# Two early expert slots in place of one in a fused attention, mixture-of-experts and FFN kernel

## The chip, the cores and the metric

The kernel runs on one core of a Trainium2 chip. The metric is the device time of one execution in microseconds (us). Engines are named as in the profile: PE is TensorE (PEld its weight loads), DVE is VectorE, ACT is ScalarE, POOL is GpSimd, SP is SyncE, which issues most transfers.

## The reference

Three stages follow one another. All inputs are float32.

```
attention:  q, k, v [4, 8, 576, 64]; scores / 8, masked by blocks of 64, softmax, times v
            -> x [2304, 512]                      (4 batches of 576 tokens, 8 heads of 64)
experts:    logits = x @ w_gate                   (8 experts)
            e(n) = argmax logits[n];  g(n) = softmax(logits[n])[e(n)]
            y[n] = g(n) * (relu(x[n] @ w1[e(n)]) @ w2[e(n)])     w1 [8, 512, 1024], w2 [8, 1024, 512]
FFN:        h = y @ w_in;  out = (relu(h) + log1p(exp(-|h|))) @ w_out    w_in [512, 2048], w_out [2048, 512]
```

So each token goes to one expert only, and which one is known when the attention of its batch, and its logits, are done.

## The kernel before

**Order of the work.** One long text, `SCHEDULE` (L45), lists some 3700 short keys in the order in which their instructions are written out. Each engine runs its own instructions in that order and waits where an input isn't there. So a key's place in the text is its place in the queue of its engine, for SP's transfers and POOL's gathers too.

**Attention.** 16 pairs of heads (4 batches, 4 pairs each). A pair `p` has keys such as `Kta.p` (transposes), `S0.p` to `S2.p` (scores), `m..p` (row maxima on DVE), `e..p` (exponentials on ACT), `T`, `h` (transposes of the weights and their copies), `V.p` (product with v), `Xa.p`, `xa.p`, `xo.p` (tokens and logits out; `xs` is stored to `xd` in device memory, L444). The pairs overlap. PSUM tile `ps2` has one buffer, which scores, token output and routing share.

**Routing.** Tokens are put into slots of 256 (`SR`), each for one expert. The early routing (`early_routing`, L610, keys `er0` to `er51`) works on the first two batches, beside the attention of the last pairs: it picks the expert with the most tokens there (`est`, L653), ranks its tokens, and makes a table of the first 256 (`giE` which token, `siE` where it goes, `gaE` its gate). Three of its steps are matmuls (count L631, ranks L636, table L641), the others short DVE operations. The late routing (`late_routing`, L693, keys `lr0` to `lr50` and `lg0` to `lg21`) starts when the attention ends; it counts all tokens that are left by expert (`oh` has 9 groups, group 0 the left tokens of the early expert), makes tables for the late slots (L750 for the token numbers, L746 for position and gate, the latter from five POOL products at L738 into `r_X`), and writes the expert of each slot and whether it differs from that of the slot ahead into `fl`.

**Slots.** Slot 0 is the early one; slots 1 to 11 are late (`NSTAT` = 12 run always; `more_slots`, L1402, runs a further one only if the late tables need it, and reads their number on every engine, L1404 in the profile). A slot `s` has these keys: `d10+s` to `d23+s` load the expert's weights, 8 x 512 KB on SP into `R` (L875, L877; from slot 1 on a load is left out when `fl` says the expert is the same); `h1i+s`, `h2i+s` on ACT (L880) and `l1i+s`, `l2i+s` on DVE (L884) split them into a high and a low part; `g0+s`, `g1+s` gather 128 tokens each on POOL (L888); `X`, `xh`, `xl` transpose and split the tokens (L903, L907, L911); `A0+s` to `A3+s` are the first layer (three products, L921 to L923), `hh`, `hl` its relu split (L927, L931); `C0+s` to `C7+s` the second layer (L941 to L943); `yo`, `sc` scale the result (L947) and scatter it (a one-column copy L951, an indirect transfer L952). Each weight part has one buffer, so slot s+1's conversions follow slot s's last use of it. The pools of the first layer's parts open near the end of the attention (`mp`), those of the second layer after it (`lp`). Keys `v0+f` to `v5+f` convert blocks of `w_in` for the FFN beside slots 1 to 4 (L840 to L845), and `vd+f` loads them (L823).

**FFN.** It follows the slots and is not touched by the change.

Of the kernel before, what the change touches and what calls it, by code (L numbers as in the profile page):

```python
# [9 lines left out]
BF16 = mybir.dt.bfloat16  # L10
I32 = mybir.dt.int32
# [11 lines left out]
SR = 256  # L23
NE, NSTAT, NSLOT = 2, 12, 16
# [89 lines left out]
h27+1 hl0+1 A1+1 d22+2 lg19 lg20 l26+1 lg21 more v0+0 l27+1 h10+2 v1+0 d23+2 h12+2 l10+2 A2+1 h14+2 l12+2 hh1+1 v2+0
h16+2 hl1+1 v0+1 v3+0 vd+2 l14+2 A3+1 v4+0 l16+2 hh2+1 v5+0 hl2+1 h11+2 v1+1 h13+2 l11+2 X0+2 h15+2 C0+1 l13+2 hh3+1
d10+3 xh0+2 l15+2 d11+3 h17+2 hl3+1 C1+1 h20+2 xl0+2 d12+3 v0+2 l17+2 X1+2 h21+2 l20+2 d13+3 C2+1 g0+3 xh1+2 l21+2
xl1+2 d20+3 g1+3 h22+2 C3+1 v2+1 l22+2 h23+2 C4+1 v3+1 vd+3 l23+2 v4+1 v1+2 C5+1 h24+2 d21+3 v5+1 l24+2 h25+2 C6+1
v2+2 l25+2 v3+2 vd+4 h26+2 C7+1 d22+3 v0+3 l26+2 v1+3 A0+2 yo0+1 sc0+1 v2+3 yo1+1 v3+3 vd+5 h27+2 v4+2 l27+2 sc1+1
v4+3 v5+2 d23+3 A1+2 v0+4 v5+3 hh0+2 v1+4 hl0+2 h10+3 v2+4 h12+3 l10+3 A2+2 h14+3 l12+3 hh1+2 l14+3 h16+3 hl1+2 v0+5
l16+3 v3+4 vd+6 A3+2 hh2+2 v1+5 v4+4 hl2+2 v0+6 v5+4 v2+5 v1+6 X0+3 C0+2 v3+5 vd+7 hh3+2 C1+2 xh0+3 v2+6 h11+3 hl3+2  # L120
h13+3 X1+3 xl0+3 h15+3 C2+2 g0+4 l11+3 xh1+3 l13+3 h17+3 d10+4 g1+4 C3+2 xl1+3 h20+3 d11+4 h21+3 l15+3 h22+3 l17+3
d12+4 C4+2 h23+3 l20+3 v4+5 d13+4 l21+3 v0+7 C5+2 l22+3 d20+4 h24+3 l23+3 h25+3 C6+2 l24+3 d21+4 l25+3 v5+5 h26+3
d22+4 C7+2 v3+6 vd+8 yo0+2 sc0+2 l26+3 A0+3 h27+3 v1+7 yo1+2 l27+3 v4+6 sc1+2 v2+7 d23+4 v5+6 v3+7 c9.-1 A1+3 hh0+3
v4+7 hl0+3 v0+8 v5+7 v1+8 h10+4 v2+8 h12+4 A2+3 hh1+3 l10+4 h14+4 hl1+3 h16+4 l12+4 l14+4 l16+4 A3+3 hh2+3 v3+8 c10.-1
hl2+3 v4+8 h11+4 v5+8 h13+4 l11+4 X0+4 h15+4 l13+4 C0+3 d10+5 hh3+3 l15+4 xh0+4 d11+5 hl3+3 h17+4 C1+3 h20+4 xl0+4
d12+5 l17+4 h21+4 X1+4 l20+4 d13+5 C2+3 g0+5 xh1+4 l21+4 xl1+4 d20+5 g1+5 h22+4 C3+3 l22+4 h23+4 C4+3 l23+4 h24+4
d21+5 C5+3 l24+4 h25+4 C6+3 l25+4 h26+4 d22+5 C7+3 l26+4 yo0+3 sc0+3 A0+4 h27+4 yo1+3 l27+4 sc1+3 d23+5 A1+4 hh0+4
hl0+4 h10+5 h12+5 l10+5 A2+4 h14+5 l12+5 hh1+4 l14+5 h16+5 hl1+4 l16+5 A3+4 hh2+4 hl2+4 h11+5 h13+5 l11+5 X0+5 h15+5
l13+5 C0+4 d10+6 hh3+4 l15+5 xh0+5 d11+6 hl3+4 h17+5 C1+4 h20+5 xl0+5 d12+6 l17+5 h21+5 X1+5 l20+5 d13+6 C2+4 g0+6
xh1+5 l21+5 xl1+5 d20+6 g1+6 h22+5 C3+4 l22+5 h23+5 C4+4 l23+5 h24+5 d21+6 C5+4 l24+5 h25+5 C6+4 l25+5 h26+5 d22+6  # L130
# [363 lines left out]
def routing_consts(tc, const, B):  # L494
# [38 lines left out]
    for n in ("sel", "nsel"):  # L533
        t(n, [128, E])
# [314 lines left out]
def moe(tc, P, K, R1, R2, xd, yd, w1, w2, w_in, HB, ident):  # L849
# [612 lines left out]
```

## Time and profile before

| | |
|---|---|
| time, median of 3 runs | 965.75 us (965.72 to 967.75) |
| the profiled execution's own time | 966.58 us |
| its span, first to last instruction | 964.9 us |
| granted TensorE clock, mean | 0.980 |
| TensorE busy | 911.9 us (95%) |
| VectorE busy | 665.9 us (69%) |
| ScalarE busy | 567.1 us (59%) |
| GpSimd busy | 142.0 us (15%) |
| moved | 144.98 MB, mean 150 GB/s |

Matmuls overlap in the array, so a row's duration is longer than the distance to the next row; where a sum is made, the distance from start to start counts. In a row of the order of time, the bracket gives the idle time of the engine ahead of it and what ended it. Slot starts, by the first L921 row after a second layer: slot 0 at 237.46 us, slot 2 at 303.33 us, slot 4 at 361.39 us, slot 5 at 384.73 us.

### The profile page before, as it was taken

How to read it: one execution, taken by the hardware profiler on the slowest of the kernel's cores; microseconds unless marked ns; L12 is line 12 of the kernel's file. 1: busy time of each engine (PE TensorE's matmuls, PEld its weight loads, DVE VectorE, ACT ScalarE, POOL GpSimd, SP SyncE). 2: the span in 40 equal slices, each digit the busy share in tenths (PEclk: the TensorE clock that was granted, in tenths of full speed). 3: DMA queues.
4: the chain of work that ended last, by engine and by line, in shares of the span. 5: the costliest groups of instructions: out<-in, count | busy, mean ns of one | idle time of the engine just before them, and what ended most of it. 6: DMA issues, size and time to landing. Idle time of an engine off the chain costs nothing.

```text
span 964.9 us, 18308 instructions
## 1 busy us (share of the span) xinstructions
PE 911.9 (95%) x6331; PEld 804.0 (83%) x6331; DVE 665.9 (69%) x1454; ACT 567.1 (59%) x1256; POOL 142.0 (15%) x183
## 2 busy tenths in 40 slices
PE   6999999999868989999999999999999989999994
PEld 4888888767757979999999887888788989999994
DVE  3776677886877966655655277777666559897873
ACT  3766766765355755555555287888788733444331
POOL 2000000010244312222221100000000003130401
PEclk9999999999979989999999999999999999999997
DMA  5973630061117773466611167556664583433421
GB/s 128 200 148 76 127 81 26 25 210 47 51 54 248 235 250 132 155 239 231 209 52 62 44 202 217 187 184 229 231 251 185 186 339 105 149 129 121 130 70 64
DMA packets 132982, 144.98 MB, mean 150 GB/s; under 512 B 70415, under 2 KB 91919, under 8 KB 132880
## 3 DMA queue, kind: packets, MB, share of 16 engines
q1 hardware_dynamic: 127600, 127.98, 42.8%
q0 software_dynamic: 5280, 15.75, 4.8%
q8 instruction: 51, 0.84, 0.4%
q14 instruction: 51, 0.42, 0.1%
HBM read 120.09 MB, written 41.96 MB: 168 GB/s over the span
## 4 chain that ended last, share of the span: by engine, by line
PE 60%; DMA 4%; DVE 3%; ACT 1%; issue 1%; SPq 0%; POOLq 0%; ACTq 0%; DVEq 0%
PE yps L941 4%; PE yps L942 4%; PE yps L943 4%; PE hps L921 3%; PE hps L922 3%; PE hps L923 3%; PE fh L1085 3%; PE fh L1084 3%; PE fh L1086 3%; PE fz L1248 2%; PE fz L1247 2%; DMA gq<-gd 2%; PE fz L1246 2%; PE fX L1085 2%; PE fX L1086 2%; PE fX L1084 2%
## 5 line engine op out<-in xcount | busy, mean ns | idle before, releaser
L921 PE MATMUL hps<-xh,H1h 128*128 128x256 f32 x384 | 110.9, 289 | 6.5 <-ACT y L947 2.9
L922 PE MATMUL hps<-xl,H1h 128*128 128x256 f32 x384 | 110.4, 288 | 5.2 <-DVE xl L911 5.2
L1209 ACT CAST ah<-sum 128x1280 fp32r<-128x1280 f32 (+1 forms) x40 | 46.3, 1156 | 113.0 <-DVE sum L1202 55.4
L923 PE MATMUL hps<-xh,H1l 128*128 128x256 f32 x384 | 110.1, 287 | 0.0
L383 ACT ACTIVATE P<-s,negm 128x448 f32<-128x448 f32 (+4 forms) x160 | 82.8, 528 | 24.4 <-DVE negm L378 24.4
L884 DVE TENSOR_TENSOR H2l<-R,H2h 128x512 fp32r<-128x512 f32 x96 | 64.8, 694 | 34.2 <-ACT H2h L880 30.8
L378 DVE TENSOR_REDUCE negm<-s 128x1 f32<-128x576 f32 (+4 forms) x160 | 67.9, 478 | 22.3 <-PE s L372 21.0
L941 PE MATMUL yps<-H2h,hh 128*128 128x512 f32 x192 | 78.3, 408 | 3.8 <-DVE hl L931 3.8
L921 PEld LDWEIGHTS hps<-xh,H1h 128*128 128x128 f32 x384 | 75.2, 196 | 7.6 <-ACT y L947 3.1
L922 PEld LDWEIGHTS hps<-xl,H1h 128*128 128x128 f32 x384 | 75.2, 196 | 6.1 <-DVE xl L911 5.7
L884 DVE TENSOR_TENSOR H1l<-R,H1h 128x512 fp32r<-128x512 f32 x96 | 66.7, 738 | 17.7 <-ACT H1h L880 16.7
L942 PE MATMUL yps<-H2h,hl 128*128 128x512 f32 x192 | 75.8, 395 | 0.0
L943 PE MATMUL yps<-H2l,hh 128*128 128x512 f32 x192 | 75.7, 394 | 0.0
L880 ACT CAST H2h<-R 128x512 fp32r<-128x512 f32 x96 | 57.5, 621 | 30.9 <-DVE H2l L884 16.3
L923 PEld LDWEIGHTS hps<-xh,H1l 128*128 128x128 f32 x384 | 75.2, 196 | 0.0
L1213 DVE TENSOR_TENSOR al<-sum,ah 128x1280 fp32r<-128x1280 f32 (+1 forms) x40 | 54.4, 1359 | 27.1 <-ACT ah L1209 26.8
L389 PE MATMUL pt<-ident,P 128*128 128x128 f32 x480 | 69.4, 281 | 3.5 <-ACT PT L394 1.5
L1275 POOL DMA_INDIRECT out_dram<-fos,OI x18 | 38.2, 2124 | 222.6 <-DVE fos L1271 183.4
L372 PE MATMUL s<-kZ,qZ 64*128 64x288 f32 (+4 forms) x576 | 64.0, 336 | 3.5 <-ACT P L383 1.6
L880 ACT CAST H1h<-R 128x512 fp32r<-128x512 f32 x96 | 55.0, 620 | 17.2 <-PE hps L922 15.1
L372 PEld LDWEIGHTS s<-kZ,qZ 64*128 64x128 f32 x576 | 53.9, 198 | 11.9 <-issue 4.7
L1248 PE MATMUL fz<-Wl,ah 128*128 128x256 f32 x216 | 61.1, 283 | 0.0
(285 smaller groups left out, 2617.5 us busy)
## 6 DMA issues: line engine op xcount, KB each, us to landing
R<-in_moe_w_dram SPq DMA_DIRECT2D x96, 512.0 KB
gd<-ft SPq DMA_DIRECT2D x64, 256.0 KB
gq<-gd SPq DMA_DIRECT2D x64, 256.0 KB
dbw<-in_moe_w_out_dram SPq DMA_DIRECT2D x32, 256.0 KB
dbl<-in_moe_w_in_dram SPq DMA_DIRECT2D x22, 256.0 KB
yg<-yd SPq DMA_DIRECT2D x4, 1026.0 KB
xd<-xs SPq DMA_DIRECT2D x16, 256.0 KB
wd<-ah SPq DMA_DIRECT2D x4, 896.0 KB
```

The source lines that it names most:

```text
L372: mm(o, lhsT=a, rhs=b, start=first, stop=last)
L383: nc.scalar.activation(t[0:n, 0:NK[c]], SC.pop((p, j, c))[0:n], AF.Exp, bias=NM.pop((p, j, c))[0:n], scale=1.0, accum_out=rs[p % 4][0:n, c ...
L389: nc.tensor.transpose(ps[:, o:o + 128], P[p, j, c][:, 128 * kc:128 * kc + 128], ident)
L880: nc.scalar.copy(HW[l, i][0], raw(l, i))
L884: TT(l_, raw(l, i), h.bitcast(F32), op=ALU.subtract)
L921: mm(a, lhsT=wh, rhs=xh, start=(k == 0), stop=False)
L922: mm(a, lhsT=wh, rhs=xl, start=False, stop=False)
L923: mm(a, lhsT=wl, rhs=xh, start=False, stop=(k == 3))
L941: mm(o, lhsT=h[:, c], rhs=wh, start=(f == 0), stop=False)
L942: mm(o, lhsT=l[:, c], rhs=wh, start=False, stop=False)
L943: mm(o, lhsT=h[:, c], rhs=wl, start=False, stop=(f == 7))
L1248: mm(o, lhsT=h, rhs=wl, start=False, stop=last)
```

## The change

The early routing now picks two experts, those with the most and the second most tokens of the first two batches (`EARLY` = 2), and makes tables for two early slots, 256 tokens each. `most(k)` and `mine(k)` are run twice; between them the first expert's count is lowered by 4096. A token's slot column is 2k or 2k+1 (`NE` = 4), the position of the second expert's tokens begins behind the first's. Group 0 of the late routing is now the left tokens of the second early expert; those of the first go back into its ordinary group. `load`, `rows` and `part` take the early tables for slots 0 and 1, so slot 1's loads carry no condition. `more_slots` counts from slot 2 on.

```diff
-NE, NSTAT, NSLOT = 2, 12, 16
+EARLY = 2
+NE, NSTAT, NSLOT = 2 * EARLY, 12, 16
...
+    def most(k):
+        return [
+            lambda: V.tensor_reduce(mc[k].unsqueeze(2), tot.rearrange("p e o -> p o e"), axis=AX.X, op=ALU.max),
+            lambda: STT(ew[k], totv, mc[k][:, 0:1], K["wts"], op0=ALU.is_ge, op1=ALU.mult),
+            lambda: V.tensor_reduce(me[k], ew[k], axis=AX.X, op=ALU.max),
+            lambda: V.tensor_scalar(K["est"][:, k:k + 1], me[k], -1.0, float(E), op0=ALU.mult, op1=ALU.add),
+            lambda: V.tensor_scalar((s0, sel)[k], ew[k], me[k][:, 0:1], None, op0=ALU.is_equal),
+        ]
+    def mine(k):
+        return [
+            lambda: TT(o2, o1, bc((s0, sel)[k].unsqueeze(1), 128, n, E), op=ALU.mult),
+            lambda: V.tensor_reduce(own[:, k].unsqueeze(2), o2, axis=AX.X, op=ALU.add),
+        ]
...
+    ] + most(0) + mine(0) + [
+        lambda: STT(totv, s0, -4096.0, totv, op0=ALU.mult, op1=ALU.add),
+    ] + most(1) + mine(1) + [
...
-        t, c = (K[n + "E"], a) if s == 0 else (K[n], 2 * (s - 1) + a)
+        t, c = (K[n + "E"], 2 * s + a) if s < EARLY else (K[n], 2 * (s - EARLY) + a)
...
-        if s:
-            e = nc.sync.value_load(fl[0:1, s - 1:s], min_val=0, max_val=E - 1)
-            kw["cond"] = nc.sync.value_load(fl[0:1, NSLOT + s - 1:NSLOT + s], min_val=0, max_val=1)
+        if s >= EARLY:
+            at = s - EARLY
+            e = nc.sync.value_load(fl[0:1, at:at + 1], min_val=0, max_val=E - 1)
+            kw["cond"] = nc.sync.value_load(fl[0:1, NSLOT + at:NSLOT + at + 1], min_val=0, max_val=1)
         else:
-            e = nc.sync.value_load(K["est"][0:1, 0:1], min_val=0, max_val=E - 1)
+            e = nc.sync.value_load(K["est"][0:1, s:s + 1], min_val=0, max_val=E - 1)
...
-                for s in range(NSTAT, NSLOT + 1):
-                    nest.enter_context(tc.If(n > s - 1))
+                for s in range(NSTAT, NSLOT + EARLY):
+                    nest.enter_context(tc.If(n > s - EARLY))
```

The order is written anew from the early routing (pair 9) to slot 4; ahead of it and from the first layer of slot 4's middle on it is the old one. What moves:

- **Early routing.** Before, `er7` to `er45` lie in one stretch from `m21.13` to `h00.13`; after, `er7` to `er24` lie beside pair 10, `er25` to `er53` beside pairs 11 and 12, `er54` (the table) to `er59` beside pair 12. The list has 69 entries in place of 52.
- **Slot 0's loads.** `wl0`, `wl4`, `wl5`, `wl6`, `wl3`, `wl7` stand beside pair 10's end, `wl2` and `wl1` beside pair 12; before, all stood beside pair 13.
- **Slot 1.** `d10+1` to `d13+1` stand beside pair 14's end, `g0+1`, `g1+1` and `d20+1` to `d23+1` at the start of slot 0. `h10+1` to `h17+1`, `l10+1` to `l16+1`, `X0+1`, `X1+1`, `xl0+1`, `xl1+1` stand among `lr5` to `lr32`, beside slot 0; before, all of slot 1 stood behind `lr50`.
- **Late routing.** Its gate and distance entries (`lg1` to `lg6`) move behind `lr47`; the table of token numbers (`lr39`) stands between `C7+0` and `A0+1` (before: between `C5+0` and `C6+0`). The gathers of slot 2 stand behind `lr50`, the five products (`lg13` to `lg17`) behind them, beside `A1+1` to `A3+1`, and the second table (`lg18`) between `A3+1` and `C0+1`. `more` stands between `C0+1` and `C1+1` (before: `A1+1` and `A2+1`).
- **Blocks of w_in.** `vd+2` stands beside `C2+1` (before `A3+1`), `vd+4` beside `A0+2` (before `C6+1`); `v0+3` stands behind `yo1+1` (before: ahead of `yo0+1`).

## Rows read from the trace of the kernel before

**Rows 1.** The page's first part: span, busy time of each engine.
```profile
span 964.9 us, 18308 instructions
PE 911.9 (95%) x6331; PEld 804.0 (83%) x6331; DVE 665.9 (69%) x1454; ACT 567.1 (59%) x1256; POOL 142.0 (15%) x183
```

**Rows 2.** Stretches: length, busy PE, PEld, DVE, ACT, POOL, clock, DMA share, GB/s.
```profile
20.00:180.00 160.00, 159.49 (x1414) 132.96 (x1413) 114.57 (x310) 112.94 (x362) 5.11 (x19) 1.00 0.51 106
...
190.00:200.00 10.00, 8.18 (x56) 4.40 (x57) 9.03 (x49) 4.37 (x16) 0.00 (x0) 0.83 0.60 184
...
260.00:270.00 10.00, 5.29 (x42) 3.70 (x38) 6.98 (x9) 6.87 (x13) 7.72 (x7) 0.92 0.19 54
270.00:280.00 10.00, 5.40 (x35) 5.35 (x36) 8.75 (x15) 4.05 (x9) 6.06 (x6) 0.57 0.25 80
300.00:310.00 10.00, 9.24 (x64) 8.45 (x62) 6.09 (x14) 2.40 (x5) 5.91 (x1) 1.00 0.91 323
...
373.00:397.00 24.00, 24.00 (x159) 21.97 (x158) 14.80 (x24) 14.28 (x27) 6.02 (x6) 1.00 0.11 38
397.00:420.00 23.00, 23.00 (x153) 21.06 (x151) 13.80 (x23) 13.30 (x24) 6.03 (x6) 1.00 0.68 230
```

**Rows 3.** TensorE in order of time, slots 0 to 5: start, length, what, idle before.
```profile
237.46 0.36 PE L921 MATMUL hps<-xh,H1h 128*128 128x256 f32 x1
...
259.56 0.97 PE L750 MATMUL lr<-r_a,r_R 128*128 128x32 bf16 x32 [0.90 <-DVE r_R L725]
...
269.17 0.58 PE L921 MATMUL hps<-xh,H1h 128*128 128x256 f32 x1 [1.55 <-ACT xh L907]
274.60 0.58 PE L922 MATMUL hps<-xl,H1h 128*128 128x256 f32 x1 [4.85 <-DVE xl L911]
...
279.19 1.56 PE L746 MATMUL lr<-r_X,r_R 128*128 128x160 bf16 x20
...
285.65 0.36 PE L921 MATMUL hps<-xh,H1h 128*128 128x256 f32 x1 [2.00 <-PEq L1404]
...
303.33 0.28 PE L921 MATMUL hps<-xh,H1h 128*128 128x256 f32 x1
...
312.14 0.39 PE L921 MATMUL hps<-xh,H1h 128*128 128x256 f32 x1 [2.90 <-ACT y L947]
...
347.92 0.80 PE L941 MATMUL yps<-H2h,hh 128*128 128x512 f32 x1 [3.81 <-DVE hl L931]
...
361.39 0.28 PE L921 MATMUL hps<-xh,H1h 128*128 128x256 f32 x1
...
384.73 0.28 PE L921 MATMUL hps<-xh,H1h 128*128 128x256 f32 x1
```

**Rows 4.** VectorE in order of time, late routing beside slot 0.
```profile
236.64 0.69 DVE L911 TENSOR_TENSOR xl<-t,xh 128x512 fp32r<-128x512 f32 x1 [0.97 <-ACT xh L907]
...
256.26 1.90 DVE L787 TENSOR_TENSOR r_a<-r_a,k_tk 128x640 bf16<-128x640 bf16 x1
...
258.82 0.68 DVE L725 TENSOR_TENSOR r_R<-k_row,r_a 128x512 bf16<-128x512 f32 x1
```

**Rows 5.** VectorE's groups by form, 265 to 267 us: busy, mean ns.
```profile
L884 DVE TENSOR_TENSOR H1l<-R,H1h 128x512 fp32r<-128x512 f32 x1 | 5.8, 5752 | 2.9 <-ACT H1h L880 2.9
```

**Rows 6.** GpSimd in order of time, 253 to 306 us.
```profile
253.38 0.24 POOL L603 CAST r_a<-r_a 128x20 bf16<-128x20 f32 x1 [14.21 <-ACT r_a L731]
...
261.79 1.06 POOL L888 DMA_INDIRECT xg<-xd,k_gi  x1 [4.31 <-DVE k_gi L802]
...
264.19 4.99 POOL L738 TENSOR_TENSOR r_X<-r_a 128x640 bf16<-128x640 bf16 x4
...
299.59 6.32 POOL L951 COPY y<-k_gi 128x1 int32<-128x1 int32 x1
```

**Rows 7.** TensorE in order of time beside the early routing.
```profile
191.86 0.66 PE L389 MATMUL pt<-ident,P 128*128 128x128 f32 x4 [1.48 <-ACT P L383]
```

**Rows 8.** ScalarE in order of time, slot 1's end.
```profile
309.78 0.43 ACT L840 ACTIVATE cvh<-dbl 128x256 f32<-128x256 f32 x1 [6.38 <-DMA dbl<-in_moe_w_in_dram]
```

More of the change, by code (lines that the diff above doesn't have):

```diff
@@ L114 @@
[L114 to L118, printed above, removed]
@@ L532, in routing_consts @@
     t("rg", [128, T])
-    for n in ("sel", "nsel"):
-        t(n, [128, E])
+    t("sel", [128, E])
     for n in ("mo", "e1"):
         t(n, [128, 1])
-    t("est", [128, 1], I32)
+    t("est", [128, 2], I32)
     for n, w in (("", 2 * NSLOT), ("E", NE)):
@@ L610, in early_routing @@
 def early_routing(nc, K, L, m, bank):
[L612 removed]
+    V, TT, STT, mm = nc.vector, nc.vector.tensor_tensor, nc.vector.scalar_tensor_tensor, nc.tensor.matmul
     n = 10
@@ L616, in early_routing @@
     ohb = m([128, E, n], BF16)
-    tot, ew = m([128, E, 1]), m([128, E])
-    mc, me = m([128, 1]), m([128, 1])
-    sel, nsel = K["sel"], K["nsel"]
-    o2, own, ownb = m([128, n, E]), m([128, n]), m([128, n], BF16)
-    C, Z, tk, s1, rw, g1, g2 = (m([128, n]) for _ in range(7))
+    tot, ew = m([128, E, 1]), [m([128, E]) for _ in range(2)]
+    totv = tot.rearrange("p e o -> p (e o)")
+    mc, me = [m([128, 1]) for _ in range(2)], [m([128, 1]) for _ in range(2)]
+    s0, sel = m([128, E]), K["sel"]
+    own, ownb = m([128, 2, n]), m([128, 2, n], BF16)
+    o2 = m([128, n, E])
+    C, Z, tk, half = (m([128, 2, n]) for _ in range(4))
+    zz, g1, g2, tks, m0 = m([128, n]), m([128, n]), m([128, n]), m([128, n]), m([128, 1])
+    rw = m([128, n])
     sl = m([128, n, NE])
@@ L634, in ranks @@
         ps = st["b"] = bank()
-        mm(ps[:, 0:n], lhsT=K["one"], rhs=ownb, start=True, stop=True)
-        mm(ps[:, 16:16 + n], lhsT=K["U"], rhs=ownb, start=True, stop=True)
+        r = ownb.rearrange("p a t -> p (a t)")
+        mm(ps[:, 0:2 * n], lhsT=K["one"], rhs=r, start=True, stop=True)
+        mm(ps[:, 32:32 + 2 * n], lhsT=K["U"], rhs=r, start=True, stop=True)
+        st["cnt"], st["bef"] = (ps[:, x:x + 2 * n].rearrange("p (a t) -> p a t", a=2) for x in (0, 32))
     def table():
@@ L659, in early_routing @@
             ranks,
-            lambda: V.tensor_tensor_scan(C, st["b"][:, 0:n], K["z"][:, 0:n], 0.0, op0=ALU.add, op1=ALU.add),
-            lambda: TT(C, C, st["b"][:, 0:n], op=ALU.subtract),
-            lambda: TT(Z, C, st["b"][:, 16:16 + n], op=ALU.add),
-        ],
-        lambda: V.scalar_tensor_tensor(tk, Z, float(128 * NE), own, op0=ALU.is_lt, op1=ALU.mult),
-        lambda: V.tensor_scalar(s1, Z, 128.0, None, op0=ALU.is_ge),
-        lambda: V.scalar_tensor_tensor(rw, s1, -128.0, Z, op0=ALU.mult, op1=ALU.add),
-        lambda: TT(sl[:, :, 1], tk, s1, op=ALU.mult),
-        lambda: TT(sl[:, :, 0], tk, sl[:, :, 1], op=ALU.subtract),
+            lambda: [V.tensor_tensor_scan(C[:, k], st["cnt"][:, k], K["z"][:, 0:n], 0.0, op0=ALU.add, op1=ALU.add) for k in range(2)],
+            lambda: TT(C, C, st["cnt"], op=ALU.subtract),
+            lambda: TT(Z, C, st["bef"], op=ALU.add),
+        ],
+        lambda: STT(tk, Z, float(SR), own, op0=ALU.is_lt, op1=ALU.mult),
+        lambda: STT(half, Z, 128.0, tk, op0=ALU.is_ge, op1=ALU.mult),
+        lambda: V.tensor_copy(slv[..., 1], half),
+        lambda: TT(slv[..., 0], tk, half, op=ALU.subtract),
+        lambda: TT(Z, Z, tk, op=ALU.mult),
+        lambda: pair(tks, tk),
+        lambda: STT(half, half, -128.0, Z, op0=ALU.mult, op1=ALU.add),
+        lambda: pair(rw, half),
         lambda: TT(Rt[0], bc(K["row"].unsqueeze(1), 128, 5, 128), bc(rw[:, 0:5].unsqueeze(2), 128, 5, 128), op=ALU.is_equal),
@@ L671, in early_routing @@
     ] + gate + [
-        lambda: V.tensor_scalar(Z, Z, float(-NT), None, op0=ALU.add),
-    ] + parts_of(nc, Z, V7[:, :, 2:4], [g1]) + parts_of(nc, K["rg"][:, 0:n], V7[:, :, 4:7], [g1, g2]) + [
+        lambda: V.tensor_scalar(m0, mc[0], float(SR), None, op0=ALU.min),
+        lambda: pair(zz, Z),
+        lambda: STT(zz, tk[:, 1], m0[:, 0:1], zz, op0=ALU.mult, op1=ALU.add),
+        lambda: V.tensor_scalar(zz, zz, float(-NT), None, op0=ALU.add),
+    ] + parts_of(nc, zz, V7[:, :, 2:4], [g1]) + parts_of(nc, K["rg"][:, 0:n], V7[:, :, 4:7], [g1, g2]) + [
         lambda: TT(X, bc(sl.unsqueeze(2), 128, n, 7, NE), bc(V7.unsqueeze(3), 128, n, 7, NE), op=ALU.mult),
```

359 lines of the change are left out of this document (181 added, 178 removed).

## The prediction
> **What bounds the kernel now.** I read the page first, then the table of stretches, then the order of time on TensorE, and last VectorE and GpSimd in the stretches where TensorE stands still. The page says that TensorE is busy 911.9 of 964.9 us [rows 1], so 53 us of idle time is all that a change of order can take, besides stretches at a lower clock. The table of stretches shows where it lies [rows 2]: in the attention (20 to 180 us) TensorE is busy 159.49 of 160 us at full clock; in 190 to 200 us, where the early tables are built, it is busy 8.18 us at a granted clock of 0.83; in 260 to 280 us it is busy 10.69 of 20 us, and the granted clock of the second half is 0.57 of 2.4 GHz, most of it at the lower level, 1.2 GHz. That hole lies between expert slot 0 and slot 1. TensorE's order of time shows it from the inside [rows 3]: slot 0 starts at 237.46, the table of the late routing (L750) waits 0.90 us for VectorE, slot 1's first product comes at 269.17, and its second only at 274.60, after 4.85 us of waiting for `xl`. Undisturbed slots take 384.73 - 361.39 = 23.34 us. Slot 1 waits because its tokens, its expert and its weights all come out of the late routing, which starts when the attention ends. VectorE sets that chain's pace: from 236.64 to 259.4 no later row of it has idle time ahead [rows 4]. Slots 2 and 3 take 361.39 - 303.33 = 58.06 us in place of 46.68; there TensorE waits 2.90 us at 312.14 and 3.81 us at 347.92 [rows 3].
>
> **The change part by part.** The sum is made against the profiled execution, 966.58 us (span 964.9 and 1.68 around it); the median of the runs shown is 0.83 us lower, and the difference found is taken off that.
>
> *Number of slots and loads.* Counted from the reference's own routing on its inputs, the eight experts have 750, 161, 186, 473, 48, 34, 202, 450 tokens, and 373 (expert 0) and 356 (expert 3) lie in the first two batches. Before: one early slot, eleven late ones. After: two early slots of 256, and 494, 161, 186, 217, 48, 34, 202, 450 left, which fill 2+1+1+1+1+1+1+2 = 10 late slots. Twelve slots run in both, at the same products and conversions. The experts come as 0 3 3 0 0 1 2 4 5 6 7 7 in place of 0 0 0 1 2 3 3 4 5 6 7 7: nine loads in place of eight, 4 MB more. Slot 1 now loads, and so does slot 6; slot 4 no longer does. I cost the extra load at nothing: a slot beside a load (397 to 420 us, transfers 0.68) keeps TensorE as full as one without (373 to 397 us, transfers 0.11) [rows 2]. Without that cover it would cost 4 MB at 323 GB/s [rows 2], 13 us.
>
> *Early tables (L610 to L689).* The list grows from 52 to 69 operations, 18 more VectorE instructions; the three TensorE steps (count, ranks, table) stay three. They are no longer pressed into half a pair but laid into three pairs. Before, the stretch holds 49 VectorE instructions in 9.03 us [rows 2], 0.18 us each, so the added 18 cost 3.3 us of VectorE. Cover: VectorE is busy 114.57 of 160 us in the attention, 3.7 us free in each pair of 13.1 us, 11 us in three. Before, the pile-up cost TensorE 1.82 us of idle time (1.48 of it in one wait, [rows 7]) and 8.18 x 0.17 = 1.4 us of clock, 3.2 us. After: at best nothing (gain 3.2), at worst as much in each of three pairs (loss 6.4). I take half of the old loss, a **gain of 1.5 us**, since in each pair VectorE's addition is about its slack. SP's early weight loads move a pair ahead; they stand in SP's queue behind the `est` values and ahead of the stores of `xs`, with a wait on VectorE that is over by then. The second loads of the attention's end (slot 1's first weights) wait on SP for slot 0's conversions; behind them is only the last stores of `xs`, which come later anyway.
>
> *Slot 0 to slot 1.* Slot 1 now needs the early tables alone, but its work and the late routing share VectorE, and on TensorE the late table (L750) still stands ahead of slot 1's first product. Before, VectorE reached the end of the last row comparison (L725) at 258.82 + 0.60 = 259.4, which is 22.8 us after 236.64 [rows 4]. After, seven H1l of slot 1 (0.60 each from start to start) and two `xl` (0.61) stand ahead of it, +5.4; the gate and distance operations move behind it, -1.3 (six small ones); and GpSimd's first product, which held L787 for 1.90 us where its twin takes 0.81, comes later, -1.1. So 236.64 + 25.8 = 262.4. TensorE, done with slot 0 near 237.46 + 23.34 = 260.8, waits for that, makes the table in 1.1 us [rows 3] and starts slot 1 at 263.5, all at full clock.
>
> *Slot 1 to slot 2.* Undisturbed: 263.5 + 23.34, the second table (L746, 1.35 us) and the read of the slot count (L1404, 2.00 us) [rows 3] give 290.2. Late next is GpSimd. Its five products for the second table need the gather of slot 2 ahead of them, and the second table stands in TensorE's queue ahead of slot 1's second layer. VectorE has the late indices 4.4 us after 262.4 (four conversions and thirteen small operations), at 266.8; two gathers (1.06 each with 0.3 between) end at 269.2, six small operations (0.24 each, 1.7 with gaps) at 270.9, five products at 4.99 / 4 = 1.25 us [rows 6] at 277.2. TensorE has finished slot 1's first layer, half a slot, at 275.2 and waits 2 us. While the products run, VectorE stands: one H1l took 5.75 us [rows 5], as long as the four products beside it. From 262.4 on it has 19.5 us of work until the last `xl` of slot 2; with 6.3 us of this hold and 3.4 us of the stop at the slot count it is done at 291.6, about when TensorE wants it. The hold goes the other way too: a GpSimd copy of one column took 6.32 us at 299.59 [rows 6] while VectorE ran without a break. I add 1 us for it. So slot 2 starts at 290.2 + 3 = 293.2 in place of 303.33, a **gain of 10.1 us**; at best 13.1, at worst 0 (the third rival).
> The Trainium skill (SBUF — State Buffer, on the shared port pair) has it that GpSimd and VectorE hold that pair for one whole instruction, and that a `tensor_tensor` with both inputs in SBUF contends with GpSimd's reads. Rows 5 and 6 agree in kind, but not in length: one VectorE operation waited through four GpSimd ones. If they took turns as the rule reads, the five products would take 5 x (1.25 + 0.60) = 9.3 us and slot 2 would start some 3 us later: 952.
>
> *Slots 2 and 3.* They lose 58.06 - 46.68 = 11.4 us now. ScalarE stood 6.38 us for a block of `w_in` [rows 8] while transfers were busy 0.91 of the time at 323 GB/s [rows 2], with the outputs of slot 1 behind it in its queue; at 347.92 the weights of slot 4 and the last blocks came together. After, slot 3 still loads in the same place, slot 4 loads nothing, and the block that ScalarE waited for stands behind slot 1's outputs. VectorE has some 45 us of work in the 46.7 us of these two slots, so it becomes the next limit. Bounds: nothing gained, or 11.4. I take a **gain of 4.8 us**, somewhat under the half, since one of two load bursts goes and VectorE has no slack. From slot 4 on the order is that of before: no change.
>
> Sum: 1.5 + 10.1 + 4.8 = 16.4; 966.58 - 16.4 = 950.2, and against the median **949.4 us**.
>
> **The rivals.**
> *A, the wait is only handed on.* The hole closes, but VectorE, full from slot 0 to slot 4, keeps the loss of slots 2 and 3 at 11.4 us: gain 11.6, 954.2. For it: VectorE's sum above; against it: 4 MB fewer in that stretch.
> *B, nearly all goes.* Slots 2 and 3 lose only 3 us and slot 2 starts at 290.2: gain 1.5 + 13.1 + 8.4 = 23, 942.8. For it: 0.91 of transfer time was what they waited for; against it: VectorE.
> *C, slower: GpSimd locked out.* VectorE runs without a break through slot 1 and keeps GpSimd from its port as at 299.59. The gathers and products then wait until VectorE runs dry, near 277.5 (it needs slot 2's tokens next); products until 288 mean that TensorE stands 12.8 us ahead of slot 1's second layer in place of 2, so 9.8 more than forecast (with the 1 us already in it). If each of the gathers for slots 3 and 4 is held 6.3 us as well, the sum is 949.4 + 9.8 + 12.6 = 971.8. It is slower from a total hold of some 19 us on. Against it: at 253.38 the small GpSimd operations took 0.24 us each [rows 6] in the midst of a full VectorE, and operations that read PSUM lie between.
> *D, a late slot too many.* If the late tokens needed eleven slots, the ones behind the static ten would run unpipelined: over 100 us more. By the counts above ten hold them (494 of 512, 450 of 512, 217 of 256).
>
> **How the numbers follow.** Forecast 0.52, A 0.23, B 0.17, C 0.05, D 0.01; 0.02 for no change by an even mix. About 0.2% (1.9 us) is what a measurement of this kernel can tell from no change. Faster takes the forecast, A and B and most of the rest between A and C: 0.93; same 0.03; slower 0.04. The range reaches past B below and over A above, with 4 us for the attention's worse side: 941 to 958.
>
> **What would show it.** Right: TensorE's wait between the slots 0 and 1 is 1 to 3 us, no clock of 0.57 there, slot 1 starting 26 us after slot 0; a wait of 1 to 4 us ahead of the L746 table, by GpSimd; twelve slots, 96 weight loads in the list as before; slots 2 and 3 together 50 to 56 us; the rest after slot 4 as long as before (603.5 us from 361.39). Wrong: slot 0 starting later than 239 (early tables held the attention up), GpSimd rows of 5 us and more between the two late tables (C), or VectorE idle in slots 2 and 3 for transfers as before (A by another cause).

## The result, and the profile after

| | before | after |
|---|---|---|
| time, median of 4 runs each on one chip | 966.04 us (965.72 to 967.75) | 948.59 us (947.75 to 950.08) |
| ratio, 95% interval | | 0.9817 [0.98, 0.9835] |
| profiled execution, its span | 966.58, 964.9 us | 950.08, 948.4 us |
| granted TensorE clock, mean | 0.980 | 0.988 |
| moved | 144.98 MB | 149.17 MB |

The forecast was 949.4 us. The two profiled executions differ by 16.5 us; the forecast's sum was 16.4. The terms of that sum are another matter. The page's head of after, against [rows 1]:

```profile
span 948.4 us, 18309 instructions
PE 906.3 (96%) x6331; PEld 800.6 (84%) x6331; DVE 661.1 (70%) x1472; ACT 567.5 (60%) x1256; POOL 136.8 (14%) x183
```

VectorE has the 18 instructions more that were counted; TensorE has as many as before. Next the stretches of after (columns as in [rows 2]):

```profile
20.00:180.00 160.00, 157.11 (x1404) 131.25 (x1403) 120.96 (x358) 110.72 (x352) 5.10 (x19) 1.00 0.59 126
...
180.00:190.00 10.00, 10.00 (x78) 6.90 (x75) 5.52 (x20) 5.88 (x18) 0.00 (x0) 0.83 0.37 107
...
260.00:270.00 10.00, 9.83 (x108) 9.32 (x107) 10.00 (x30) 4.63 (x8) 4.41 (x4) 1.00 0.15 54
270.00:280.00 10.00, 4.83 (x41) 4.65 (x40) 7.25 (x10) 4.89 (x9) 9.65 (x11) 0.98 0.22 56
280.00:290.00 10.00, 6.62 (x33) 5.52 (x33) 1.28 (x5) 0.25 (x1) 1.75 (x2) 0.68 0.55 163
...
290.00:345.00 55.00, 55.00 (x344) 49.67 (x343) 53.02 (x107) 41.24 (x84) 19.80 (x15) 1.00 0.64 208
```

The hole at 260 us is gone, and a smaller one stands at 275 to 288 us, in the middle of slot 1, with a granted clock of 0.68 behind it. From 290 to 345 us TensorE never stands, with VectorE busy 53.02 of 55 us beside it. TensorE in order of time, as in [rows 3]; L956 is the first layer's first product, L784 and L780 are the two late tables, L976 the second layer:

```profile
236.88 0.36 PE L956 MATMUL hps<-xh,H1h 128*128 128x256 f32 x1
...
261.82 0.96 PE L784 MATMUL lr<-r_a,r_R 128*128 128x32 bf16 x32 [0.17 <-DVE r_R L759]
...
262.63 0.36 PE L956 MATMUL hps<-xh,H1h 128*128 128x256 f32 x1
...
281.80 2.83 PE L780 MATMUL lr<-r_X,r_R 128*128 128x160 bf16 x20 [6.97 <-POOLq L1440]
...
288.49 0.47 PE L976 MATMUL yps<-H2h,hh 128*128 128x512 f32 x1 [1.58 <-PEq L1440]
...
298.58 0.28 PE L956 MATMUL hps<-xh,H1h 128*128 128x256 f32 x1
...
321.92 0.28 PE L956 MATMUL hps<-xh,H1h 128*128 128x256 f32 x1
...
345.23 0.28 PE L956 MATMUL hps<-xh,H1h 128*128 128x256 f32 x1
```

Slot 1 starts 25.75 us after slot 0, with a table wait of 0.17 us between them. It then waits 6.97 us for the second table, whose releaser is GpSimd. GpSimd in order of time shows why (L987 scatters slot 0's result, L923 gathers slot 2's tokens, L772 makes the products):

```profile
262.31 1.45 POOL L987 DMA_INDIRECT yd<-y,k_siE  x1 [21.59 <-ACT H2h L915]
...
266.95 1.38 POOL L987 DMA_INDIRECT yd<-y,k_siE  x1 [2.70 <-ACT hh L962]
268.63 1.09 POOL L923 DMA_INDIRECT xg<-xd,k_gi  x1 [0.30 <-PE hps L958]
270.03 1.45 POOL L923 DMA_INDIRECT xg<-xd,k_gi  x1 [0.31 <-issue]
271.49 1.00 POOL L603 CAST r_a<-r_a 128x20 bf16<-128x20 f32 x1
...
274.63 7.12 POOL L772 TENSOR_TENSOR r_X<-r_a 128x640 bf16<-128x640 bf16 x5
```

From 266.95 to 281.75 GpSimd has no gap longer than 0.31 us. Its gathers were forecast for 266.8. VectorE has their indices ready sooner, at 265.5:

```profile
265.35 0.18 DVE L836 TENSOR_SCALAR k_gi<-r_a 128x32 int32<-128x32 f32 x1
```

The gathers start at 268.63 all the same, because slot 0's second scatter stands ahead of them in GpSimd's queue. That scatter itself stood for 2.70 us. The profile puts this down to ScalarE; in a_table2_late it puts the same wait (3.09 us) down to the transfer of the first scatter.

Put against the profiled execution of before, the 16.5 us come from: the attention 0.58 (slot 0 starts at 236.88 in place of 237.46), slot 0 to slot 2 4.17 (61.70 in place of 65.87), slots 2 and 3 11.41 (46.65 in place of 58.06), and 0.34 behind slot 4 (603.17 in place of 603.51).

### The profile page after: what moved, and what is told of

Its sections match the earlier page's. It is cut to its first block, busy times and chain, and to the rows that moved or that the text cites. A ratio compares the mean times of both kernels' runs of the same rounds, so it can differ in the third digit from the quotient of the medians.

```text
span 948.4 us, 18309 instructions
## 1 busy us (share of the span) xinstructions
PE 906.3 (96%) x6331; PEld 800.6 (84%) x6331; DVE 661.1 (70%) x1472; ACT 567.5 (60%) x1256; POOL 136.8 (14%) x183
## 2 busy tenths in 40 slices
DMA packets 134646, 149.17 MB, mean 157 GB/s; under 512 B 70543, under 2 KB 92047, under 8 KB 134544
## 4 chain that ended last, share of the span: by engine, by line
PE 64%; DMA 2%; DVE 1%; ACT 1%; issue 0%; POOLq 0%; SPq 0%; DVEq 0%; ACTq 0%
PE yps L976 4%; PE yps L978 4%; PE yps L977 4%; PE hps L957 4%; PE hps L958 4%; PE hps L956 4%; PE fh L1121 3%; PE fh L1120 3%; PE fh L1122 3%; PE fz L1284 2%; PE fz L1283 2%; DMA gq<-gd 2%; PE fz L1282 2%; PE fX L1121 2%; PE fX L1122 2%; PE fX L1120 2%
## 5 line engine op out<-in xcount | busy, mean ns | idle before, releaser
L956 PE MATMUL hps<-xh,H1h 128*128 128x256 f32 x384 | 109.0, 284 | 0.0
L976 PE MATMUL yps<-H2h,hh 128*128 128x512 f32 x192 | 77.6, 404 | 1.6 <-PEq L1440 1.6
L956 PEld LDWEIGHTS hps<-xh,H1h 128*128 128x128 f32 x384 | 73.6, 192 | 0.6 <-ACT xh L942 0.2
L919 DVE TENSOR_TENSOR H1l<-R,H1h 128x512 fp32r<-128x512 f32 x96 | 63.3, 696 | 14.3 <-ACT H1h L915 13.3
```

Source lines behind the costliest of these rows:

```text
L919: TT(l_, raw(l, i), h.bitcast(F32), op=ALU.subtract)
L956: mm(a, lhsT=wh, rhs=xh, start=(k == 0), stop=False)
L976: mm(o, lhsT=h[:, c], rhs=wh, start=(f == 0), stop=False)
```

## The experiments

In the diffs, `put(keys, behind)` takes these keys out of `SCHEDULE` and puts them behind the key named; each kernel starts from the one in its label (a: after, b: before). A length from slot to slot is that of one profiled execution. Slot 0 starts between 235.12 and 236.96 us in the eight profiles made from after and between 235.41 and 238.00 us in the six made from before, though the attention's order is the same in each group; so a difference of a microsecond or two between two profiles can be chance. One table holds what was measured: the time, its ratio to the kernel before on the same chip with its 95% interval, and from the profile the lengths from slot to slot and ScalarE's waits of over 1 us for a block of `w_in` (`dbl`) from 290 us to slot 4.

| run | us | ratio [95%] | 0 to 1 | 1 to 2 | 2+3 | 0 to 4 | ScalarE's waits for `dbl` |
|---|---|---|---|---|---|---|---|
| before | 966.04 | | 31.71 | 34.16 | 58.06 | 123.93 | 6.38, 1.83, 7.02 |
| after | 948.59 | 0.9817 [0.98, 0.9835] | 25.75 | 35.95 | 46.65 | 108.35 | 1.82 |
| a_slot1_behind | 960.87 | 0.9953 [0.9935, 0.997] | 36.55 | 35.00 | 47.05 | 118.60 | 2.34, 1.49, 1.50 |
| a_scatter_late | 950.44 | 0.9833 [0.9807, 0.9858] | 25.66 | 37.22 | 46.68 | 109.56 | 1.59, 1.97 |
| a_table2_late | 950.49 | 0.9834 [0.9811, 0.9857] | 25.74 | 32.84 | 50.59 | 109.17 | 2.79 |
| a_table2_late_no_lo2 | 946.91 | 0.9802 [0.9777, 0.9826] | 25.74 | 32.21 | 48.60 | 106.55 | 1.29 |
| a_products_dve | 947.03 | 0.9806 [0.9785, 0.9827] | 25.74 | 31.28 | 48.98 | 106.00 | 1.75 |
| a_force_load4 | 952.28 | 0.9842 [0.981, 0.9874] | 25.75 | 37.98 | 46.66 | 110.39 | 2.00, 1.10 |
| a_block7_ahead_load4 | 950.23 | 0.9836 [0.9802, 0.9869] | 25.74 | 37.28 | 46.67 | 109.69 | 1.24, 1.66 |
| b_skip_load4 | 959.37 | 0.9929 [0.9901, 0.9957] | 31.73 | 33.90 | 50.35 | 115.98 | 4.95, 1.85 |
| b_block3_behind | 965.58 | 1.0 [0.9983, 1.0018] | 31.72 | 33.72 | 55.13 | 120.57 | 4.44, 1.32, 1.60, 6.06 |
| b_table2_x7 | 973.07 | 1.0076 [1.005, 1.0102] | 31.71 | 42.94 | 54.33 | 128.98 | 5.05, 1.53, 6.79 |
| b_block7_behind | 969.0 | 1.0039 [1.0021, 1.0057] | 31.73 | 35.93 | 58.08 | 125.74 | 5.45, 1.44, 10.89 |
| b_blocks27_behind | 976.23 | 1.01 [1.0074, 1.0125] | 31.70 | 36.20 | 64.91 | 132.81 | 11.35, 1.92, 10.03 |

### Is it the preparation of slot 1 beside slot 0?

**a_slot1_behind.** Slot 1's gathers, second-layer loads, conversions, transposes and the start of its first layer go back behind the late routing; its first four loads stay early.

```diff
+SCHEDULE = put('g0+1 g1+1 d20+1 d21+1 h10+1 ... l20+1 l21+1 l22+1 A0+1 d10+2'.split(), 'lr50')
```

> The changed kernel with the early tables and early first-layer weights as they are, but slot 1's gathers, second-layer loads, conversions and token transposes put behind the late indices, as the kernel before has them. Theory O (the hole ahead of slot 1 closes because slot 1 is prepared beside slot 0): slot 1 starts at 267 to 271 in place of 262.6, and with what follows the time is 952 to 957. Theory T (it is enough that slot 1's tokens and expert are known early): slot 1 starts by 264.5 and the time is 947 to 950.

TensorE in order of time, slot 1's start:

```profile
270.53 0.48 PE L948 MATMUL t<-ident,xg 128*128 128x128 f32 x1 [8.93 <-DMA xg<-xd,k_giE]
...
273.46 0.58 PE L966 MATMUL hps<-xh,H1h 128*128 128x256 f32 x1
```

The hole is back: slot 1 starts 36.55 us after slot 0 (25.75 in after), and 12.3 us of the gain are lost. This is theory O, beyond its bounds (slot 1 starts at 273.46 us, the time is 960.87). It costs more than was expected since slot 1 doesn't get shorter for it (35.00 against 35.95; its table still waits 3.33 us). So it is the early preparation that closes the hole. Slots 2 and 3 keep 47.05 us, so their gain does not come from an early slot 1.

### What the second table's wait is worth

**a_scatter_late.** Slot 0's scatter goes behind the products.

```diff
+SCHEDULE = put("sc0+0 sc1+0".split(), "lg17")
```

> The changed kernel, with slot 0's two scatters behind the five products in GpSimd's queue; now they stand ahead of slot 2's gathers. Theory W: the train starts 1.5 to 2.5 us earlier, the wait ahead of the second table falls from 6.97 to 4.5 to 5.5 us and the time to 946 to 947. Theory D: the wait falls as well, but slot 4 starts within 1 us of before, 948 to 949.

The wait falls only from 6.97 to 5.62, and the slots 0 to 4 take 109.56 us, 1.2 more than in after: the stop at the slot count is 2.23 us in place of 1.58, and slot 1 is 1.3 us longer. The products begin 3.1 us earlier (271.53), but they take 8.48 us in place of 7.12, while six H1l of VectorE beside them take 7.57 us where three take 1.92 undisturbed. The scatter is part of the wait; no gain from taking it out can be seen, and the interval of the time overlaps that of after.

**a_table2_late.** The second table, with the read of the slot count and the block conversions beside it, goes behind slot 1's fifth second-layer step.

```diff
+SCHEDULE = put("lg18 lg19 lg20 lg21 more v0+0 v1+0 v0+1 v2+0 v3+0 vd+2 v4+0 v5+0 v1+1".split(), "C4+1")
```

> The changed kernel, with the second table of the late routing, the read of the slot count and the first block conversions moved from ahead of slot 1's second layer to behind its fifth step (C4+1). Theory W (the 6.97 us wait ahead of that table is GpSimd's train alone; nothing else is late): the wait falls under 0.5 us, no slow clock in slot 1, slot 2 starts 7 to 9.5 us earlier, near 290, and the time is 939.5 to 942. Theory V (VectorE would be late anyway with slot 2's preparation, as the forecast's sum had it): slot 2 starts at 294 to 296, the time is 944 to 946.

TensorE in order of time:

```profile
281.54 1.54 PE L790 MATMUL lr<-r_X,r_R 128*128 128x160 bf16 x20 [1.21 <-POOLq L1450]
...
286.83 0.77 PE L986 MATMUL yps<-H2h,hh 128*128 128x512 f32 x1 [3.74 <-PEq L1450]
...
301.59 0.39 PE L966 MATMUL hps<-xh,H1h 128*128 128x256 f32 x1 [2.00 <-ACT y L992]
```

Of the wait 5.8 us are gone, and all of it comes back: 2.2 us in the stop at the slot count, most of the rest in slot 2, which waits for slot 1's outputs and runs at 0.83 of the clock from 300 to 310 us. Slots 0 to 4 take 109.17 us, 0.8 more than in after. Neither theory had this: the time is 950.49 us, where the less hopeful one said 944 to 946.

**a_table2_late_no_lo2.** The same, and slot 2's 16 low-part subtractions are left out (slot 1's values stand in their place; both slots have expert 3).

```diff
+            if n[0] == "h" or s != 2:
+                (hi if n[0] == "h" else lo)(int(n[1]), i)
```

> The changed kernel with the second table behind C4+1 as in the run before, and slot 2's sixteen subtractions for the low parts of its weights left out (slot 2 has slot 1's expert here, so the low parts are there already): 9.6 us less for VectorE, none less for ScalarE and the transfers. Theory D with VectorE as the limit: slot 2 no longer loses 3.7 us, slot 4 starts 5 to 8 us earlier than 344.29, the time is 941 to 944. Theory D with the transfers as the limit: slot 2 still waits for blocks of w_in, slot 4 starts within 2 us, the time is 947 to 950.

With 16 x 0.60 = 9.6 us less for VectorE the slots 0 to 4 take 106.55 us, 2.6 less than a_table2_late, though the stop at the slot count grew to 4.87. So part of what came back was VectorE's work, and part was not: it falls between the two theories, nearer to the one with the transfers (slot 4 starts at 343.51 us, the time is 946.91).

**a_products_dve.** The five products and the six small operations ahead of them go from GpSimd to VectorE.

```diff
-nc.gpsimd.tensor_tensor(X[:, :, i], sl, bc(v...
+nc.vector.tensor_tensor(X[:, :, i], sl, bc(v...
-V5[:, :, 0:2], [g1], True)
+V5[:, :, 0:2], [g1])
-V5[:, :, 2:5], [g1, g2], True)
+V5[:, :, 2:5], [g1, g2])
```

> The changed kernel, with the five products for the second late table and the six small operations ahead of them on VectorE in place of GpSimd. Theory W (the 6.97 us wait ahead of that table is GpSimd's train, and nothing else is behind): VectorE takes about 0.8 us for a product, 5.4 us in all, and no longer stands for GpSimd; the wait falls to 1 to 3 us, slots 2 and 3 stay at 46.7 us, the time falls by 4 to 6 us to 943 to 945. Theory D (VectorE's and the transfers' work from slot 0 to slot 4 sets slot 4's start, and the wait only takes up its slack): slot 4 starts at most 2 us earlier, slots 2 and 3 take 49 to 52 us, the time is 946.5 to 949.

TensorE in order of time:

```profile
276.97 2.82 PE L780 MATMUL lr<-r_X,r_R 128*128 128x160 bf16 x20 [3.38 <-DVE r_X L772]
...
299.57 0.39 PE L956 MATMUL hps<-xh,H1h 128*128 128x256 f32 x1 [0.98 <-ACT y L982]
303.54 0.38 PE L956 MATMUL hps<-xh,H1h 128*128 128x256 f32 x1 [0.83 <-DVE hl L966]
```

And one of the products, now on VectorE:

```profile
268.93 0.85 DVE L772 TENSOR_TENSOR r_X<-r_a 128x640 bf16<-128x640 bf16 x1
```

The wait halves: a product takes VectorE 0.81 to 0.85 us, GpSimd 7.12 / 5 = 1.42. Slot 1 is 4.7 us shorter, and 2.3 of that come back in slot 2. This is close to theory D (slots 2 and 3 take 48.98 us, the time is 947.03). The slots 0 to 4 take 106.00 us, 2.35 less than in after; of the versions that compute everything this has the lowest median, 1.6 us below after, though the intervals of the two ratios overlap. The profiled execution of after took 950.08 us, 1.5 over its median, that of a_products_dve its median.

### Why slots 2 and 3 lose nothing

**a_force_load4.** Slot 4 loads its expert again, as it must in the order before.

```diff
+            if s != 4:
-            kw["cond"] = nc.sync.value_load(...)
+                kw["cond"] = nc.sync.value_load(...)
```

> The changed kernel, but slot 4 always loads its weights (the same expert as slot 3's, so the same numbers): 4 MB more beside slot 3. Theory 1 (slots 2 and 3 lost 11.4 us before because slot 4's load came on top of the blocks of w_in, and the change lost that load): slots 2 and 3 together go from 46.65 us back to 50 to 54, the time from 948.6 to 952 to 956. Theory 2 (the new order of the blocks, with conversion v0+3 behind slot 1's outputs, does it): 46.7 us and 948.6, within 1 us.

**b_skip_load4.** In the kernel before, slot 4 loads nothing (its tokens get slot 3's expert).

```diff
+        if s == 4:
+            return
```

> The kernel before, with slot 4's load left out (slot 4's tokens get slot 3's expert): the mirror image. Theory 1: slot 3 no longer waits, slots 2 and 3 go from 58.06 us to 51 to 53, the time from 966 to 959 to 961. Theory 2: 58 us and 966, within 1 us.

The two disagree. In the old order, without this load slot 3 takes 23.33 us and loses nothing, and slots 2 and 3 together fall from 58.06 to 50.35. In the new order the load costs these slots nothing (46.66). The median of a_force_load4 is 3.7 us above that of after, with overlapping intervals; its profile is longer in slot 1 (37.98 in place of 35.95 us), ahead of that load. The theory that the missing load alone is the cause falls: the load hurts these slots only in the old order.

**b_block3_behind.** The conversion of the block that ScalarE waited for [rows 8] goes behind slot 1's outputs, where the new order has it.

```diff
+SCHEDULE = put("v0+3 v1+3 v2+3".split(), "yo1+1")
```

> The kernel before, with the first three steps of the conversion of block 3 of w_in moved behind slot 1's second output in the queues. Theory 2: the wait of 2.90 us in slot 2 and its slow clock go, slots 2 and 3 take 53 to 54 us, the time is 961 to 962. Theory 1: ScalarE still has to wait for the block ahead of the next relu, so slot 2 loses as much a little later, 58 us and 966, within 1 us.

TensorE's wait for `y` is gone, and one of 4.35 us for `hl` is in its place: the same conversion, still waiting 4.44 us for its block, now stands ahead of `hh`. The profile's slots 2 and 3 are 2.9 us shorter, where theory 2 said 4 to 5; the time is the same, as theory 1 had it.

**b_table2_x7.** The second table is made seven times, which holds TensorE up within slot 1's first layer (the table stands between `A0+1` and `A1+1` in the order before).

```diff
-            for i in range(T): ... start=(i == 0), stop=(i == T - 1)
+            for i in range(7 * T): ... (i % T) ...
```

> The kernel before, with the 20 products of the second late table done seven times over (the same result), so that TensorE has 8.2 us more to do in slot 1 (1.36 us each time). Theory P (slots 2 and 3 lost their 11.4 us because transfers and VectorE were behind TensorE there; a stop of TensorE ahead of them is paid back): slots 2 and 3 together fall from 58.06 us to 49 to 52 and the time stays at 966, within 2 us. Theory Q (their loss comes of how slots 2 and 3 themselves are ordered): they keep 57 to 58 us and the time is 973 to 975.

Slot 1 is 8.8 us longer, slot 2 loses 3.0 us less, and slot 3 still waits 4.15 us for `hl`. The two together keep 54.33 us, between the theories; the time, 973.07, is Q's. A pause there lets some 3.7 of the 11.4 us catch up.

**b_block7_behind, b_blocks27_behind, a_block7_ahead_load4.** The place of the blocks 7 and 2 in SP's queue: two kernels made from before have block 7, or both, behind the weights, as after has them, and one made from after has block 7 ahead of the weights, as before has it.

```diff
+SCHEDULE = put("vd+7 v0+7".split(), "d20+4")
```


> The kernel before, with the load and the first conversion step of block 7 of w_in (vd+7, v0+7) moved in SP's and ScalarE's queues from ahead of slot 4's first-layer weights to behind the first of its second-layer weights, where the changed kernel has them. Theory S (a block's load that waits for a free buffer holds the weights behind it in SP's queue, and slot 3 then waits for them): slot 4's weights are asked for 5 us earlier and more, slot 3 takes 23.5 to 26 us in place of 30.1, slot 2 is as before, the time is 959 to 962. Theory L (slot 4's load alone is too much there): slot 3 keeps 29 to 31 us and the time 965 to 967.


```diff
+SCHEDULE = put("vd+2 v0+2".split(), "d13+3")
+SCHEDULE = put("vd+7 v0+7".split(), "d20+4")
```


> As the run of block 7, and block 2's load and first step moved behind slot 3's first-layer weights as well. Theory S: slot 2 also loses less, 24 to 26 us in place of 28.0, slots 2 and 3 together take 47.5 to 52 us, the time is 956 to 960. Theory L: both stay, 57 to 59 us together and 965 to 967.


```diff
+            if s != 4:          (as in a_force_load4)
+SCHEDULE = put("v2+5 v3+5 vd+7".split(), "C0+2")
```


> The changed kernel with slot 4's load forced (as in the earlier run, which lost nothing in slots 2 and 3), and block 7's load, with the two conversion steps that it needs, put ahead of slot 4's weights, as the kernel before has it. Theory S: slot 3 waits again, 27 to 31 us in place of 23.3, the time is 952 to 957. Theory L and every theory in which the slots ahead set it: slot 3 stays under 24.5 us, 948 to 953.

The first two are slower, the third loses nothing in slots 2 and 3, so the place of these two blocks in SP's queue alone is not the cause. The first two are slower than both theories said. In them the block's load moved far back and its conversion only a little, so they are no test of the new order, where the conversions lie later too. ScalarE in order of time in b_block7_behind:

```profile
337.78 0.43 ACT L850 ACTIVATE cvh<-dbl 128x256 f32<-128x256 f32 x1 [10.89 <-DMA dbl<-in_moe_w_in_dram]
```

What they do show is the mechanism, with its size: a conversion that stands for its block holds slot 2's outputs behind it, and TensorE waits 7.75 us for `y`. The last column of the table fits this: each run in the old order has a wait of 4.4 us or more there, none in the new order one of 3 us.

Where the margin comes from can be read off the block that held slot 3 up, block 8, which both orders load right behind slot 4's seventh weight part. SP's queue in the kernel before (L875 and L877 are the weights, L823 the blocks):

```profile
326.10 0.36 SPq L875 DMA_DIRECT2D R<-in_moe_w_dram  x1
328.32 4.14 SPq L875 DMA_DIRECT2D R<-in_moe_w_dram  x3
333.98 4.25 SPq L877 DMA_DIRECT2D R<-in_moe_w_dram  x3
338.27 2.70 SPq L823 DMA_DIRECT2D dbl<-in_moe_w_in_dram  x2
```

ScalarE in the kernel before:

```profile
344.52 0.43 ACT L840 ACTIVATE cvh<-dbl 128x256 f32<-128x256 f32 x1 [7.02 <-DMA dbl<-in_moe_w_in_dram]
```

SP's queue in a_force_load4, which has the same loads:

```profile
320.18 0.40 SPq L913 DMA_DIRECT2D R<-in_moe_w_dram  x1
320.62 1.63 SPq L857 DMA_DIRECT2D dbl<-in_moe_w_in_dram  x2
323.11 1.70 SPq L913 DMA_DIRECT2D R<-in_moe_w_dram  x2
324.85 1.48 SPq L857 DMA_DIRECT2D dbl<-in_moe_w_in_dram  x2
```

ScalarE there, at the conversion of the same block:

```profile
333.06 0.76 ACT L874 ACTIVATE cvh<-dbl 128x256 f32<-128x256 f32 x2
```

Before, the block is issued at 338.27, 7.0 us after slot 3's start (331.31), and ScalarE wants it at 344.52 - 7.02 = 337.50, 6.2 us after that start. In the new order it is issued 1.2 us after slot 3's start (323.65) and wanted 9.4 us after it, since its conversion stands one step of the first layer later. So both ends moved: the issue 5.8 us earlier, the need 3.2 us later. The loads run ahead from slot 3 on: its first is issued 7.7 us ahead of slot 2's start before (295.65), 18.6 us in after (280.01, where TensorE stood for the table). One run in the old order comes near to telling the two apart. In b_skip_load4, ScalarE wants block 8 6.3 us after slot 3's start (330.41), as in the kernel before, but the block's two halves are issued at about 323.2 and at 332.40, since no weights stand ahead of it. ScalarE does not wait for it:

```profile
336.72 0.76 ACT L840 ACTIVATE cvh<-dbl 128x256 f32<-128x256 f32 x2
```

So there the earlier issue was enough without the later need, with 4 MB less traffic beside it. For the new order this is a reading of traces: no run moved block 8, or gave the old order the earlier loads alone, so how much each of the two gives there stays open.

## Why the prediction was right in its sum and wrong in its terms

- **Slot 0 to slot 1: right.** Forecast 26.04 us from start to start; measured 25.75. Of that a wait of 1 to 3 us was forecast and 0.17 measured, since TensorE leaves slot 0's second layer 24.4 us after slot 0's start in place of 23.34, and VectorE is done at 261.7 in place of 262.4. The clock of 0.57 is gone, and a_slot1_behind shows the cause.
- **Attention: about right, perhaps too large.** Forecast a gain of 1.5 us, measured 0.58 in one pair of profiles. With slot 0's start averaged over all profiles of each group (236.3 and 237.2 us) it is 0.9; the starts within a group spread by about 2 us, so how far the forecast missed is not shown. The early tables' cost is spread, not gone: TensorE is busy 157.11 of 160 us from 20 to 180 us in place of 159.49 [rows 2], and the granted clock of 0.83 now stands at 180 to 190 us.
- **Slot 1 to slot 2: the failed step.** Forecast 29.7 us, measured 35.95, so the gain to slot 2 was 4.17 and not 10.1. The step was "Late next is GpSimd ... and waits 2 us", with 1 us more for a held GpSimd; the wait is 6.97. The chain of GpSimd was right and its sum was not: slot 0's scatter ahead of the gathers (268.63 in place of 266.8, with the indices there at 265.5), the two gathers 2.9 us in place of 2.4, the six small operations 3.1 us in place of 1.7, the five products 7.12 in place of 6.25. The forecast listed what POOL's work needs, and not what stands ahead of it in POOL's queue. Of the 6.25 us, the wait is 3.97; the stop at the slot count is 0.42 shorter than taken; most of the other 2.7 lies in the lower clock behind the wait (0.68 in 280 to 290 us), for which the sum had nothing. Nor was VectorE held for 6.3 us in after: three H1l beside the products took 3.02 us in place of 1.9, and then VectorE stood 7.17 us for the table.
- **Slots 2 and 3: mis-sized the other way.** Forecast a gain of 4.8 us, measured 11.41, the whole loss. The view was right (a block that ScalarE waits for, with slot 1's outputs behind it), one reason was wrong (the missing load of slot 4 is not needed: a_force_load4), and so was that slot 3 "still loads in the same place" (its first load is issued 18.6 us ahead of slot 2's start in place of 7.7). VectorE, which was to keep half of the loss as "the next limit", is busy 53.02 of 55 us and TensorE still never waits. Rival A falls with that, as far as the kernel after goes; in a_table2_late and a_products_dve, where slot 1 ends earlier, slot 2 does wait for `y` and `hl`.
- **The rest: right.** Behind slot 4 603.17 us were measured in place of 603.51; the list of transfers has 96 weight loads; the extra 4 MB cost nothing that can be seen. Rival C did not come: GpSimd's longest row between the tables is 1.45 us besides the products. No slot ran behind the static twelve (D).

That the sum of 949.4 came so close to 948.59 is luck: two errors of 5.9 and 6.6 us with opposite signs. They may not be wholly independent: TensorE's longer wait in slot 1 is also time in which slot 3's loads ran ahead, and where the wait was cut (a_table2_late, a_products_dve), slots 2 and 3 lost 2.3 to 3.9 us again. Slot 3's first load was issued 15.2 and 13.9 us ahead of slot 2 in these two; in a_slot1_behind, 17.5 us ahead, they lost 0.4.

## What to carry to other kernels

Before costing a chain on a side engine, write down its queue from the last instruction that is done to the one you need, transfers for other work included; the inputs' arrival is only a lower bound. When a stop is moved into a stretch that runs full, look at what runs ahead during it and what is late behind it: here half or all of what a shorter slot 1 gave was handed back in slots 2 and 3. Judge a transfer that is wanted within a burst by two times, its issue and the time at which its reader's queue comes to it. And compare a forecast with the result term by term: here the sum was right to 1 us with two terms wrong by some 6 us each.

## What the runs showed of the hardware that was not expected

- VectorE and GpSimd hold each other up to very different lengths. The Trainium skill (SBUF — State Buffer, "SBUF: two separate sides") has the port pair that the two share held for one whole instruction. In [rows 5] an H1l took 5.75 us beside four products; in after the three H1l at the start of the products lost 1.1 us together, and in a_scatter_late three others took 4.54 us in place of 1.92. The first of GpSimd's small conversions, of the same form, took 1.00 us in after and 0.24 us in [rows 6]. One length for a hold fits none of these kernels.
- The stop of TensorE where the slot count is read has no fixed price: 0.96, 1.58, 1.82, 2.15, 2.23, 3.74 and 4.87 us in seven of the kernels, for the same read; VectorE stood 4.06 us there in after. The two longest were where the read stood in the middle of the second layer.
- A wait of 7 us on TensorE was followed by the lower clock level, and in some kernels a short stop behind it was followed by it again. In after the granted clock is 0.50 from 282 to 286 us and 1.00 from 288 us on, behind the stop of 1.58 us at the slot count. In a_force_load4, with the same work and a stop of 2.15 us, it is 1.00 from 286 to 288 us and 0.50 again from 290 to 292 us. From the table to slot 2 that makes 16.78 us in after and 18.79 us in a_force_load4, 1.4 us more than the longer stop explains.
